# Negated row maxima and their rounded parts made by four reduce operations

## The chip, the core and the metric

The kernel runs on one core of a Trainium2 chip. The metric is the device time of one execution in microseconds (us). A core has five engines that run their own instruction streams and wait for each other through semaphores: TensorE (PE, matmuls; PEld are its weight loads), VectorE (DVE), ScalarE (ACT), GpSimd (POOL) and SyncE (SP, which here issues DMAs). SBUF is the on-chip working memory, PSUM the memory that matmuls write. In the profile L12 is line 12 of the kernel.

## What is computed

The reference mixes two branches of the same shape by a gate. Branch A is a Fourier transform of x (2048 x 512), written as matmuls; branch B is multi-head attention with 32 heads of 16 columns.

```python
def _A_ref(x, dft_seq_re, dft_seq_im, dft_hid_re, dft_hid_im):
    a = jnp.einsum("bsd,ed->bse", x, dft_hid_re)
    b = jnp.einsum("bsd,ed->bse", x, dft_hid_im)
    y = jnp.einsum("ts,bse->bte", dft_seq_re, a) - jnp.einsum("ts,bse->bte", dft_seq_im, b)
    return y

def _B_ref(x, wqkv, wo):
    ...
    scores = jnp.einsum("bhqd,bhkd->bhqk", q, k) * scale
    p = _softmax(scores, axis=-1)
    o = jnp.einsum("bhqk,bhkd->bhqd", p, v)
    return (lambda x, *d: x.transpose(*d))(o, 0, 2, 1, 3).reshape(B, S, D) @ wo

x = A_x
g = _sigmoid((x * gate_w).sum(-1, keepdims=True))
a = _A_ref(x, A_dft_seq_re, A_dft_seq_im, A_dft_hid_re, A_dft_hid_im)
b = _B_ref(x, B_wqkv, B_wo)
return g * a + (1 - g) * b
```

The attention weights are scaled so that the scores are large. The softmax therefore needs the true maximum of each row of scores before the exponential.

## The kernel before

Numbers that must be exact are carried as two float32r parts, a rounded one and the rest, so that three matmuls make one exact product.

The 32 heads are 16 pairs. For a pair p the queries and keys stand in the tiles `qs` and `ks` (two buffers each, p % 2), 64 rows for each head of the pair: 48 rows hold the parts of q or k, and two more rows of `qs`, 48 and 49 within each head's half, hold the negated row maximum in two parts, against rows of ones in `ks`. So a score matmul of a later step already delivers score minus maximum, and ScalarE only takes the exponential.

Each pair goes through two passes over its scores. In the first, `a_tile` (L285) multiplies 128 queries by 512 keys into a PSUM tile `a` (L291), and VectorE reduces it to one maximum per query (L293), into `mx`. After the 64 tiles of half a pair (`hf`, 1024 queries of both heads), two steps are put on a list, `deferred` (L297): `m_parts` and `m_rows`. `m_parts` takes the maximum over the four key blocks, negated, into `nm` (L302), its float32r rounding into `nhl[:, 0]`, and the rest into `nhl[:, 1]`. `m_rows` transposes the 32 numbers of each partition (L313) and sends them by eight DMAs (L319) into the two rows of `qs`. In the second pass `scores` (L778) makes the scores less their maximum (L791) with keys across the partitions, and the exponential `pt` (L792). `pv` (L825) multiplies it by the values into the PSUM tile `acc` (L839), and `evacuate` (L807) copies `acc` and adds it up on POOL (L819).

All of this runs woven into branch A. A section, `segment` (L946), takes its order from a written pattern: `d` matmuls (L465) of the Fourier branch on one half of the TensorE's rows, beside `a` and `s` matmuls on the other half, and at `|` the value matmuls. The long middle part is made of 192 sections with the pattern FULL (L916), each with 8 `a` tiles, 8 `s` tiles and two calls of `pv` at its end. PSUM banks are given by number in that pattern. An `a` matmul waits until the bank it writes was read by VectorE (L293) or by ScalarE (L792).

At the end of a FULL section (L990) everything deferred is run at once, and `full_now` is true: all of `m_parts` goes to VectorE, where L306 makes the rounding as a maximum of a number with itself, and L309 the rest. In the other sections the same is split: the first reduce on VectorE, a cast (L308) and a subtraction on POOL, and the transpose one section or part later. There are 32 halves of pairs; 24 of them come to this point in FULL sections.

POOL's own work in the full sections: the split of the Fourier matrices into two parts (`c_split`, L449 a cast and L450 a subtraction, each over 128 x 512), the sum of value tiles (L819), in the second half of the branch a sum with an earlier result (L524), and four of the eight DMAs of `m_rows`. Its instructions run in the order in which they were written. The transpose waits for the eight DMAs that read the same `mt` buffer before; an instruction with many waits is preceded by EVENT_SEMAPHORE instructions of its engine's queue, two waits each.

Of the kernel before, what the change touches and what calls it, by code (L numbers as in the profile page):

```python
# [9 lines left out]
F32 = mybir.dt.float32  # L10
F32R = mybir.dt.float32r
AF = mybir.ActivationFunctionType  # L12
ALU = mybir.AluOpType
AX = mybir.AxisListType

P = 128
# [15 lines left out]
def mix_kernel(ctx: ExitStack, tc: tile.TileContext, xa_t, xa, wqkv, w_hid, w_seq, wo, gate_w, out):  # L32
# [5 lines left out]
    nc = tc.nc  # L38
# [32 lines left out]
    const = ctx.enter_context(tc.tile_pool(name="const", bufs=1))  # L71
# [19 lines left out]
    ng = const.tile([P, NT], F32, name="ng")  # L91
    omg = const.tile([P, NT], F32, name="omg")
    mx = [const.tile([P, 2, NT, 4], F32, name=f"mx{i}") for i in range(2)]
    nm = [const.tile([P, 16], F32, name=f"nm{i}") for i in range(2)]
    nhl = [const.tile([P, 2, 16], F32R, name=f"nhl{i}") for i in range(2)]
    mt = [const.tile([P, 32], F32, name=f"mt{i}") for i in range(2)]

# [184 lines left out]
    full_now = False  # L282
    a_left = {}

    def a_tile(i, h, ps=None, bank=None):  # L285
        p, j = divmod(i, 64)
        qt, kb = divmod(j, 4)
        if ps is None:
            ps = psA.tile([P, 512], F32, "a", bank)
        r = slice(64 * h, 64 * h + (64 if p else 48))  # L290
        nc.tensor.matmul(ps, qs[p % 2][r, qt * P:(qt + 1) * P], ks[p % 2][r, kb * 512:(kb + 1) * 512],  # L291
                         start=True, stop=True)
        user = nc.vector.tensor_reduce(mx[p % 2][:, h, qt, kb:kb + 1], ps, AX.X, ALU.max)  # L293
        hf = j // 32
        a_left[p, hf] = a_left.get((p, hf), 64) - 1
        if not a_left[p, hf]:
            deferred.extend((partial(m_parts, p, hf), partial(m_rows, p, hf)))  # L297
        return user

    def m_parts(p, hf):  # L300

        nc.vector.tensor_reduce(nm[hf].rearrange("p (q h) -> p h q", h=2), mx[p % 2][:, :, 8 * hf:8 * hf + 8, :],  # L302
                                AX.X, ALU.max, negate=True)
        t = nhl[hf]
        if full_now:
            nc.vector.tensor_tensor(t[:, 0], nm[hf], nm[hf], ALU.max)  # L306
        else:
            nc.gpsimd.tensor_copy(t[:, 0], nm[hf])  # L308
        (nc.vector if full_now else nc.gpsimd).tensor_tensor(t[:, 1], nm[hf], t[:, 0].bitcast(F32), ALU.subtract)  # L309

    def m_rows(p, hf):

# [568 lines left out]
    for hf in range(2):  # L881
        for ct in range(4):
            n = 3 if hf and ct == 3 else 4
# [11 lines left out]
    one, two, three = [(psD, "d")], [(psS, "s"), (psD, "d")], [(psS, "s"), (psA, "a"), (psD, "d")]  # L895
# [195 lines left out]
```

## Time and profile before

| | us |
|---|---|
| median of three runs | 1675.19 (1674.93 to 1675.42) |
| the profiled execution | 1675.2 |
| its span, first to last instruction | 1673.4 |
| TensorE busy | 1663.6 (99% of the span) |
| VectorE busy | 1383.1 (83%) |
| ScalarE busy | 1242.9 (74%) |
| POOL busy | 660.1 (39%) |

The page groups instructions by source line, with their count, busy time, mean duration and the idle time ahead of them. Other views give single instructions in order of time (start and duration in us, then engine, line, operation, output tile and input tiles, shapes), the minimum, median and maximum duration of one line's instructions, and the busy time of every engine in a stretch of the span. VectorE operations that need nothing from each other overlap by some 0.08 us in the records, so a start is read against the next start rather than against an end. The granted TensorE clock is 0.999 of full speed in the mean.

### The profile page before, as it was taken

What the parts mean: (1) busy time and instruction counts of PE and PEld (TensorE: products, weight loads), DVE (VectorE), ACT (ScalarE), POOL (GpSimd) and SP (SyncE); (2) the same over time, 40 slices, a digit from 0 to 9 for tenths busy, and PEclk for the clock granted to TensorE, in tenths of its full rate; (3) what the DMA queues carried; (4) which work ended last, traced back from release to release, by engine and by line L of the source; (5) the groups of instructions that cost most, each with busy time, mean ns of one, the idle gap of its engine ahead of it and who ended that gap; (6) DMA issues with size and microseconds to landing.
All of it is one profiled execution on the core that took longest, in us unless ns stands there. A gap on an engine that the chain in (4) does not pass through costs nothing.

```text
span 1673.4 us, 34595 instructions
## 1 busy us (share of the span) xinstructions
PE 1663.6 (99%) x13040; PEld 1023.8 (61%) x13040; DVE 1383.1 (83%) x2337; ACT 1242.9 (74%) x2423; POOL 660.1 (39%) x688
## 2 busy tenths in 40 slices
PE   9999999999999999999999999999999999999998
PEld 7888855556666666656665665655665666545544
DVE  5439888888888888888888888888888888888954
ACT  5212377788888878887888787877888888788886
POOL 0202112234444456444444466554545456421110
PEclk9999999999999999999999999999999999999999
DMA  8963610414141443414156434324142535452114
GB/s 291 348 157 122 176 19 2 70 33 84 45 91 46 75 113 78 91 45 84 39 97 247 95 112 109 73 63 77 52 84 65 105 103 121 140 184 40 38 30 140
DMA packets 82689, 166.70 MB, mean 100 GB/s; under 512 B 19664, under 2 KB 20158, under 8 KB 78510
## 3 DMA queue, kind: packets, MB, share of 16 engines
q1 hardware_dynamic: 78282, 163.53, 38.5%
q8 instruction: 103, 1.69, 0.5%
q0 software_dynamic: 3808, 0.30, 0.2%
q14 instruction: 64, 0.52, 0.1%
q10 hardware_dynamic: 432, 0.66, 0.1%
HBM read 109.14 MB, written 54.65 MB: 98 GB/s over the span
## 4 chain that ended last, share of the span: by engine, by line
PE 98%; DVE 1%; DMA 0%; ACT 0%; issue 0%; DVEq 0%
PE acc L839 27%; PE d L465 27%; PE a L291 17%; PE s L791 14%; PE s L379 3%; PE s L411 1%; PE acc L799 1%; PE d L379 1%; PE s L106 1%; PE a L106 1%; PE a L108 1%; PE s L108 1%; PE s L107 1%; PE a L107 1%; DVE mx L293 1%; PE s L465 1%
## 5 line engine op out<-in xcount | busy, mean ns | idle before, releaser
L293 DVE TENSOR_REDUCE mx<-a 128x1 f32<-128x512 f32 x2026 | 1256.5, 683 | 177.3 <-PE a L291 151.8
L792 ACT ACTIVATE pt<-s 128x512 f32<-128x512 f32 x2006 | 1023.4, 622 | 70.9 <-PE s L791 59.9
L291 PE MATMUL a<-ks,qs 64*128 64x512 f32 (+1 forms) x2026 | 726.7, 405 | 2.2 <-DVE mx L293 2.2
L791 PE MATMUL s<-qs,ks 64*128 64x512 f32 (+1 forms) x2006 | 690.4, 400 | 0.0
L465 PE MATMUL d<-xab,ch 64*128 64x512 f32 x2016 | 645.9, 395 | 0.0
L291 PEld LDWEIGHTS a<-ks,qs 64*128 64x128 f32 (+1 forms) x2026 | 366.3, 184 | 217.2 <-issue 128.7
L839 PE MATMUL acc<-pt,vt 128*17 128x512 f32 (+1 forms) x3968 | 486.7, 598 | 0.0
L819 POOL TENSOR_TENSOR oe<-oe,part 128x512 f32<-128x512 f32 x169 | 218.3, 1292 | 507.7 <-ACT part L818 502.6
L791 PEld LDWEIGHTS s<-qs,ks 64*128 64x128 f32 (+1 forms) x2006 | 365.6, 185 | 55.1 <-issue 16.8
L465 PE MATMUL d<-xab,cl 64*128 64x512 f32 x1008 | 397.9, 395 | 0.0
L465 PEld LDWEIGHTS d<-xab,ch 64*128 64x128 f32 x2016 | 367.1, 184 | 26.5
L818 ACT COPY part<-acc 128x512 f32<-128x512 f32 x169 | 99.2, 587 | 183.0 <-PE acc L839 181.1
L839 PEld LDWEIGHTS acc<-pt,vt 128*17 128x17 f32 (+1 forms) x3968 | 91.6, 101 | 214.3 <-issue 151.5
L465 PEld LDWEIGHTS d<-xab,cl 64*128 64x128 f32 x1008 | 185.9, 184 | 13.7
L450 POOL TENSOR_TENSOR cl<-craw,ch 128x512 fp32r<-128x512 f32 x126 | 162.1, 1286 | 10.1
L465 PE MATMUL d<-wre,xab 64*128 64x512 f32 x336 | 90.5, 402 | 0.0
L449 POOL CAST ch<-craw 128x512 fp32r<-128x512 f32 x126 | 76.8, 609 | 16.5 <-PE s L791 14.4
L465 PEld LDWEIGHTS d<-wre,xab 64*128 64x128 f32 x336 | 58.9, 185 | 38.7 <-issue 23.3
L319 POOL DMA_DIRECT2D qs<-mt x119 | 67.0, 568 | 27.0 <-PE a L291 9.5
L465 PE MATMUL d<-wo_hl,o_hl 64*128 64x512 f32 (+1 forms) x246 | 68.2, 409 | 0.0
L465 PEld LDWEIGHTS d<-wo_hl,o_hl 64*128 64x128 f32 (+1 forms) x246 | 42.3, 185 | 29.7 <-issue 12.1
L483 POOL CAST xab<-y 128x512 fp32r<-128x512 f32 x16 | 9.8, 611 | 127.3 <-ACT y L481 99.1
(172 smaller groups left out, 1042.7 us busy)
## 6 DMA issues: line engine op xcount, KB each, us to landing
craw<-w_seq SPq DMA_DIRECT2D x128, 256.0 KB
qk<-hl SPq DMA_DIRECT2D x32, 512.0 KB
qs<-qk SPq DMA_DIRECT2D x96, 128.0 KB
ks<-qk SPq DMA_DIRECT2D x96, 128.0 KB
b<-hl SPq DMA_DIRECT2D x16, 512.0 KB
xab<-b SPq DMA_DIRECT2D x16, 512.0 KB
o<-oe SPq DMA_DIRECT2D x62, 128.0 KB
oh<-nh SPq DMA_DIRECT2D x12, 512.0 KB
```

The lines of the kernel that those rows point to most:

```text
L291: nc.tensor.matmul(ps, qs[p % 2][r, qt * P:(qt + 1) * P], ks[p % 2][r, kb * 512:(kb + 1) * 512], start=True, stop=True)
L293: user = nc.vector.tensor_reduce(mx[p % 2][:, h, qt, kb:kb + 1], ps, AX.X, ALU.max)
L319: (nc.gpsimd if own else nc.sync).dma_start(rows.rearrange("v (q b c) -> v b q c", q=8, b=4)[:, b], mt[hf][32 * b + h:32 * b + 32:2])
L379: i = nc.tensor.matmul(ps, st[r], mv[r], start=not half and not j, stop=half == 1 and j == 11)
L449: nc.gpsimd.tensor_copy(h1, raw)
L450: nc.gpsimd.tensor_tensor(l1, raw, h1.bitcast(F32), ALU.subtract)
L465: i = nc.tensor.matmul(self.ps, st[r], mv[r], start=not self.begun, stop=stop)
L791: nc.tensor.matmul(ps, ks[p % 2][rr, kt * P:(kt + 1) * P], qs[p % 2][rr, q0:q0 + 512], start=True, stop=True)
L792: return nc.scalar.activation(pts[u][:, 2 * qb + h], ps, AF.Exp, bias=0.0, scale=DH ** -0.5)
L818: nc.scalar.copy(part[0], acc)
L819: nc.gpsimd.tensor_tensor(total, total, part[0], ALU.add)
L839: i = nc.tensor.matmul(acc[32 * j:32 * j + width], v[:, 16 * h:16 * h + width], pt[:, j], start=begin, stop=done or close)
```

## The change

`nm` gets a second column. In the FULL sections `m_parts` reduces `mx` three times: negated into the first column of `nm` (float32), not negated and rounded to float32r into the second column, and negated and rounded into `nhl[:, 0]`. A fourth reduce adds the two columns: minus the maximum plus its rounding, which is the rest, into `nhl[:, 1]`. L306 and L309 are gone. In the other sections the work stays as it was, but reads the first column of the wider `nm`. In the instruction streams as built, the second and the third reduce carry no wait, the fourth waits for the second, and the transpose waits for the fourth and for the same DMAs as before. Line numbers behind this place grow by four.

```diff
-    nm = [const.tile([P, 16], F32, name=f"nm{i}") for i in range(2)]
+    nm = [const.tile([P, 16, 2], F32, name=f"nm{i}") for i in range(2)]
...
     def m_parts(p, hf):
 
-        nc.vector.tensor_reduce(nm[hf].rearrange("p (q h) -> p h q", h=2), mx[p % 2][:, :, 8 * hf:8 * hf + 8, :],
-                                AX.X, ALU.max, negate=True)
-        t = nhl[hf]
+        m, n, t = mx[p % 2][:, :, 8 * hf:8 * hf + 8, :], nm[hf], nhl[hf]
+        parts = [(n[:, :, 0], True)]
         if full_now:
-            nc.vector.tensor_tensor(t[:, 0], nm[hf], nm[hf], ALU.max)
+            parts += [(n[:, :, 1].bitcast(F32R), False), (t[:, 0], True)]
+        for out, negate in parts:
+            nc.vector.tensor_reduce(out.rearrange("p (q h) -> p h q", h=2), m, AX.X, ALU.max, negate=negate)
+        if full_now:
+            with nc.allow_low_precision(reason="two terms, rounded once"):
+                nc.vector.tensor_reduce(t[:, 1], n, AX.X, ALU.add)
         else:
-            nc.gpsimd.tensor_copy(t[:, 0], nm[hf])
-        (nc.vector if full_now else nc.gpsimd).tensor_tensor(t[:, 1], nm[hf], t[:, 0].bitcast(F32), ALU.subtract)
+            nc.gpsimd.tensor_copy(t[:, 0], n[:, :, 0])
+            nc.gpsimd.tensor_tensor(t[:, 1], n[:, :, 0], t[:, 0].bitcast(F32), ALU.subtract)
```

## The prediction

> **What bounds the kernel now.** I read the page first, then the waits of TensorE, then the lines of the changed helper, then its surroundings in order of time, and last the length of the stretches that hold it. Page and TensorE waits:
>
> ```profile
> span 1673.4 us, 34595 instructions
> ...
> PE 98%; DVE 1%; DMA 0%; ACT 0%; issue 0%; DVEq 0%
> ...
> PE a L291 <- DVE mx L293: 2.2, 4, 0.6
> ```
>
> TensorE sets the end: 98% of the chain that ended last is its own. The only VectorE work it is seen waiting for in the long middle part is the row maximum of a score tile (L293), four times, 2.2 us in all. A busy TensorE can still run slower than it might, so what a late maximum really costs is taken from lengths below, not from this idle time.
>
> The lines that the change touches, each with min/median/max in ns:
>
> ```profile
> L302 DVE TENSOR_REDUCE nm<-mx x32: 207/209/221, 171.7 to 1609.6; 128x16 f32<-128x64 f32 x32
> L306 DVE TENSOR_TENSOR nhl<-nm x24: 174/175/1041, 367.6 to 1431.0; 128x16 fp32r<-128x16 f32 x24
> L309 DVE TENSOR_TENSOR nhl<-nm,nhl x24: 174/175/519, 367.8 to 1432.1; 128x16 fp32r<-128x16 f32 x24
> L313 DVEq EVENT_SEMAPHORE  x115: 21/50/50, 280.9 to 1609.8; - x115
> L313 DVE STREAM_TRANSPOSE mt<-nhl x32: 200/211/214, 174.2 to 1610.8; 128x32 f32<-128x32 f32 x32
> ```
>
> The reduce and the transpose always take the same time; the two two-input operations, 16 numbers per partition, take 175 ns or up to six times that. Two of the 24 places in order of time (start, duration; VectorE, then VectorE and POOL of the second):
>
> ```profile
> 413.43 0.21 DVE L302 TENSOR_REDUCE nm<-mx 128x16 f32<-128x64 f32 x1
> 413.67 0.18 DVE L306 TENSOR_TENSOR nhl<-nm 128x16 fp32r<-128x16 f32 x1
> 413.88 0.18 DVE L309 TENSOR_TENSOR nhl<-nm,nhl 128x16 fp32r<-128x16 f32 x1
> 414.28 0.21 DVE L313 STREAM_TRANSPOSE mt<-nhl 128x32 f32<-128x32 f32 x1 [0.23 <-DMA craw<-w_seq]
> 414.42 3.69 DVE L293 TENSOR_REDUCE mx<-a 128x1 f32<-128x512 f32 x6
> ```
>
> ```profile
> 1012.99 0.21 DVE L302 TENSOR_REDUCE nm<-mx 128x16 f32<-128x64 f32 x1
> 1013.24 1.04 DVE L306 TENSOR_TENSOR nhl<-nm 128x16 fp32r<-128x16 f32 x1
> 1014.31 0.52 DVE L309 TENSOR_TENSOR nhl<-nm,nhl 128x16 fp32r<-128x16 f32 x1
> 1014.86 0.21 DVE L313 STREAM_TRANSPOSE mt<-nhl 128x32 f32<-128x32 f32 x1
> 1015.00 3.68 DVE L293 TENSOR_REDUCE mx<-a 128x1 f32<-128x512 f32 x6
> ```
>
> ```profile
> 1012.96 1.28 POOL L524 TENSOR_TENSOR y<-y,yr 128x512 f32<-128x512 f32 x1
> 1014.19 0.61 POOL L449 CAST ch<-craw 128x512 fp32r<-128x512 f32 x1
> ```
>
> In the second, L306 ends at 1014.28, 0.04 us after POOL's L524 (1014.24); L309 starts inside POOL's cast and ends at 1014.83, 0.03 us after it (1014.80). L302 ran wholly inside L524 and kept its 0.21. So a small two-input operation that meets a running POOL operation lasts until that one ends, and a one-input reduce does not.
>
> What a late L293 costs TensorE, in lengths from the start of one section's value matmuls (L839) to the next section's. The columns are stretch, us, then busy time by engine:
>
> ```profile
> 371.53:411.82 40.29, 40.29 (x338) 24.44 (x337) 34.76 (x57) 32.64 (x65) 17.06 (x17) 1.00 0.47 80
> 411.82:417.61 5.79, 5.79 (x50) 3.77 (x48) 5.49 (x13) 4.64 (x10) 3.33 (x6) 1.00 0.16 51
> 457.92:463.91 5.99, 5.99 (x50) 3.41 (x49) 5.69 (x13) 5.38 (x11) 5.35 (x8) 1.00 0.46 137
> 734.61:740.62 6.01, 6.01 (x51) 3.44 (x49) 5.71 (x13) 5.39 (x11) 5.38 (x8) 1.00 0.45 137
> 873.08:879.05 5.97, 5.97 (x51) 3.42 (x49) 5.67 (x13) 5.35 (x11) 5.33 (x8) 1.00 0.44 134
> 1011.40:1018.22 6.82, 6.26 (x51) 3.42 (x49) 6.72 (x13) 5.40 (x11) 6.62 (x8) 1.00 0.40 114
> 1150.58:1157.40 6.82, 6.26 (x51) 3.41 (x49) 6.72 (x13) 5.38 (x11) 5.45 (x7) 1.00 0.37 117
> 1157.40:1197.58 40.18, 40.18 (x337) 24.68 (x336) 34.77 (x57) 32.65 (x65) 18.74 (x20) 1.00 0.18 54
> 1197.58:1203.74 6.16, 6.16 (x51) 3.48 (x49) 5.51 (x13) 4.77 (x10) 4.37 (x6) 1.00 0.16 46
> 1290.01:1296.82 6.81, 6.24 (x50) 3.40 (x48) 6.71 (x13) 5.37 (x11) 5.43 (x7) 1.00 0.36 113
> 1429.17:1435.95 6.78, 6.24 (x53) 3.42 (x51) 6.68 (x13) 5.34 (x11) 5.41 (x7) 1.00 0.23 79
> ```
>
> Seven sections without the helper last 40.29 us, 5.756 each (the section ends are those of the value matmuls in the order of time). Sections with it stand at every eighth place, 24 of them, as L306's count says. From the first reduce to the next L293 the helper holds VectorE for 0.99 us at 413.43 (section 5.79, excess 0.03) and for 2.01 at 1012.99 (section 6.82, excess 1.06): 1.02 later there, 1.03 longer the section. So up to about 0.95 us VectorE catches up (eight maxima of 0.6 us, from start to start, in 5.756), and beyond that each microsecond late is a microsecond of TensorE.
>
> **The change, part by part.** Call the start of the first reduce T. Now: L306 at T+0.24, L309 at T+0.45, transpose at T+0.85, next L293 at T+0.99. The 0.40 between L309 and the transpose is more than L309's 0.18: four of VectorE's semaphore waits (the L313 DVEq row) stand there, and they follow L309's issue whatever it takes. The built order has the same waits for the transpose after the change.
>
> *Removed:* L306 and L309, 24 times each. With them goes what seven of the 24 lose to POOL: 5.99 + 6.01 + 5.97 + 6.82 + 6.82 + 6.81 + 6.78 = 45.20, less 7 x 5.756 = 40.29, is 4.9 us. A little of it is given back today: the seven sections behind a long stall last 40.18 against 40.29, 0.11 less. Four long ones give at most 0.5; I take 0.3. Net 4.6.
>
> *Added:* two more reduces over the same 64 numbers (R2, R3) and one over 16 pairs (R4). R2 and R3 wait for nothing; R4 waits for R2, not for R3, which writes another tile. No row shows an independent small reduce behind a reduce in these sections; the nearest are these, and the gap L302 to L306 with a wait (0.24):
>
> ```profile
> 195.51 0.17 DVE L772 TENSOR_SCALAR ng<-g 128x16 f32<-128x16 f32 x1
> 195.59 0.17 DVE L773 TENSOR_SCALAR omg<-g 128x16 f32<-128x16 f32 x1
> ...
> 1478.08 0.22 DVE L302 TENSOR_REDUCE nm<-mx 128x16 f32<-128x64 f32 x1
> 1478.21 3.07 DVE L293 TENSOR_REDUCE mx<-a 128x1 f32<-128x512 f32 x5
> ```
>
> So a step is 0.08 at least and 0.24 at most; I take 0.13, since that row is the same reduce with an independent one behind it. R2 at T+0.13, R3 at T+0.26, R2 done at 0.13 + 0.24 = T+0.37, and the engine is free for R4 at T+0.39. R4 lasts between 0.17 and 0.21 (16 and 64 inputs), under the 0.40 of the four waits, so it costs nothing itself; were those waits gone, it would cost its 0.2. Transpose at T+0.79, next L293 at T+0.93: 0.06 before today's undisturbed case, though one operation more is issued. For the sixteen undisturbed sections (24 less the seven and the one below) that is worth what they still exceed 5.756 by, 0.03 in the row of 411.82: at most 16 x 0.03 = 0.5; I take 0.3.
>
> The Trainium skill speaks against this part: "VectorE: DVE Perf Modes", section "The DRAIN you can't avoid", says that the next operation does not start until the pipe is empty, and its "Rules for kernel authors" say to minimize the number of operations. By that rule the step would be the longer one and rival B would hold; the 0.13 row does not bear it out.
>
> *Kept:* the section at 1197.58 is 0.40 long with no stall of a two-input operation:
>
> ```profile
> 1199.64 0.17 DVE L309 TENSOR_TENSOR nhl<-nm,nhl 128x16 fp32r<-128x16 f32 x1
> 1200.39 0.21 DVE L313 STREAM_TRANSPOSE mt<-nhl 128x32 f32<-128x32 f32 x1 [0.58 <-DVE nhl L309]
> ```
>
> Its transpose comes 0.75 behind L309 instead of 0.40, so the waits between lasted longer. They stay; I count no gain there (bounds 0 and 0.4).
>
> The eight places outside the full sections keep their cast and subtraction on POOL, reading every other number of a wider tile, behind other work: nothing, and if uncovered some 0.2 us. The transposes' DMAs (four on SP and, where POOL issues, four there) start up to 0.9 us earlier in stalled places; POOL reaches its own only after L449, which ends at 1014.80 either way. Nothing else is moved past a queue.
>
> *Sum:* 4.6 + 0.3 = 4.9 us. The profiled execution took 1675.2 (1.8 outside its span), which is also the median of before: 1675.2 - 4.9 = **1670.3 us**.
>
> **The rivals.**
>
> *B, slower.* The four reduces run one behind the other, 0.24 apart. R4 at T+0.73, transpose at T+1.13, next L293 at T+1.27, 0.28 later than an undisturbed place today, so an excess of 0.31 in 24 sections, 7.4 us, against today's 4.6 + 24 x 0.03 = 5.3: 2.1 slower, **1677.3**. It decides once the next L293 is later than T+0.99 + 4.6/24 = T+1.18. For it: every dependent pair is 0.24 or 0.21 apart. Against: the 0.13 row.
>
> *C, the stall stays.* It is not the second SBUF input but the fp32r output that waits for POOL; R2, R3 and R4 write fp32r too. Then only the 0.3 is left: **1674.9**. For it: L306 and L309 write fp32r and the unharmed L302 does not, and no row shows a reduce that does. Against it, a two-input operation of another stage, with one input in PSUM (tile s) and an fp32r output, inside a POOL operation:
>
> ```profile
> 39.65 0.69 DVE L103 TENSOR_TENSOR hl<-s,hl 128x512 fp32r<-128x512 f32 x1 [0.45 <-ACT hl L102]
> 39.21 1.29 POOL L103 TENSOR_TENSOR wv<-raw,wv 128x512 fp32r<-128x512 f32 x1 [37.90 <-ACT wv L102]
> ```
>
> It ends at 40.34, before POOL's at 40.50, so the output alone does not wait. The Trainium skill, "SBUF — State Buffer", section "SBUF: two separate sides", says the same in general: VectorE operations with two SBUF inputs or in a two-port mode take the pair of ports shared with GpSimd, whole operation against whole operation. By it C falls; for a reduce that writes fp32r no run here shows it yet.
>
> *D, half overlap.* R4 midway between T+0.39 and T+0.73: next L293 at T+1.10, 0.11 later, 24 x 0.11 = 2.6 lost of 4.6: 2.0 gained, **1673.2**.
>
> **How the numbers follow.** Chances: forecast 0.70, B 0.07, C 0.06, D 0.12, and 0.05 for what I don't see, most of it slower. The forecast's own range goes from everything at 5.756 with nothing given back and the 0.4 gone too (4.9 + 0.5 + 0.4 = 5.8, 1669.4) to 1671.6, where the step is 0.17. To hold 8 in 10 it must take in D: 1669.0 to 1674.0. A change of 0.2% (3.4 us, what can be told apart here) is reached by the forecast and the better edge of D: faster 0.72. C, B's centre and most of D are within it: 0.22. Slower by more: 0.06, from B with a longer step and the unseen.
>
> **What would show it.** In the profile after: no small VectorE operation in these places over 0.25 us; R2 and R3 0.13 apart; R4 near T+0.39; transpose 0.40 behind it; next L293 near T+0.93; the stretches that begin with the seven stalled sections at 5.76 to 5.80; TensorE's 2.2 us of waiting for L293 gone. Wrong would be reduces of 0.4 to 1 us (C), starts 0.24 apart (B), a stall that moves to the transpose, or sections at 5.76 with the time lost after the full sections instead.

## The result and the profile after

| | before | changed |
|---|---|---|
| median of 8 runs, us | 1675.06 (1674.55 to 1675.5) | 1670.16 (1669.9 to 1670.3) |
| span of the profiled execution, us | 1673.4 | 1668.1 |

The ratio of the changed kernel's time to the one before is 0.997, with a 95% interval of 0.9961 to 0.9979: 4.9 us faster, as forecast (1670.3).

From the page of the changed kernel, the chain that ended last; and TensorE's waits in the list of waits:

```profile
PE 99%; DMA 0%; DVE 0%; DVEq 0%; issue 0%
...
PE d L178 <- DVE xab L173: 1.1, 1, 1.1
PE s L243 <- DVE xab L164: 0.2, 1, 0.2
```

TensorE now waits for VectorE only at the start of the kernel; the row with L293, 2.2 us, is gone. The small operations, line by line (count, then min/median/max in ns; L307 has the first three reduces, L310 the fourth, L317 is the transpose that was L313):

```profile
L307 DVE TENSOR_REDUCE nm<-mx x56: 208/211/222, 171.3 to 1604.1; 128x16 f32<-128x64 f32 x32, 128x16 fp32r<-128x64 f32 x24
L307 DVE TENSOR_REDUCE nhl<-mx x24: 205/208/211, 367.3 to 1426.6; 128x16 fp32r<-128x64 f32 x24
L310 DVE TENSOR_REDUCE nhl<-nm x24: 178/179/184, 367.4 to 1426.7; 128x16 fp32r<-128x32 f32 x24
L317 DVE STREAM_TRANSPOSE mt<-nhl x32: 199/211/214, 173.8 to 1605.4; 128x32 f32<-128x32 f32 x32
```

None exceeds 222 ns in any place, with fp32r outputs or without; 37 of these reduces ran wholly inside a POOL operation. The section that stood first among the long ones, in order of time (VectorE, then POOL; two reduces are merged in the first row):

```profile
1012.15 0.34 DVE L307 TENSOR_REDUCE nm<-mx 128x16 f32<-128x64 f32 x2
1012.40 0.20 DVE L307 TENSOR_REDUCE nhl<-mx 128x16 fp32r<-128x64 f32 x1
1012.53 0.18 DVE L310 TENSOR_REDUCE nhl<-nm 128x16 fp32r<-128x32 f32 x1
1012.89 0.21 DVE L317 STREAM_TRANSPOSE mt<-nhl 128x32 f32<-128x32 f32 x1 [0.18 <-DVE nhl L310]
1013.03 0.65 DVE L293 TENSOR_REDUCE mx<-a 128x1 f32<-128x512 f32 x1
```

```profile
1012.13 1.29 POOL L528 TENSOR_TENSOR y<-y,yr 128x512 f32<-128x512 f32 x1
```

POOL's sum runs from 1012.13 to 1013.42 and covers all of it, and every operation keeps its length. The next maximum starts 0.88 us behind the first reduce; it was 2.01. In most of the 24 places it is 0.91. The first rows below show one of them; in the rows behind, at 459, the transpose comes late and the maximum with it, 1.28 us behind the first reduce:

```profile
413.03 0.34 DVE L307 TENSOR_REDUCE nm<-mx 128x16 f32<-128x64 f32 x2
...
413.94 0.65 DVE L293 TENSOR_REDUCE mx<-a 128x1 f32<-128x512 f32 x1
```

```profile
459.13 0.34 DVE L307 TENSOR_REDUCE nm<-mx 128x16 f32<-128x64 f32 x2
...
459.50 0.18 DVE L310 TENSOR_REDUCE nhl<-nm 128x16 fp32r<-128x32 f32 x1
460.27 0.21 DVE L317 STREAM_TRANSPOSE mt<-nhl 128x32 f32<-128x32 f32 x1 [0.59 <-DVE nhl L310]
460.41 1.25 DVE L293 TENSOR_REDUCE mx<-a 128x1 f32<-128x512 f32 x2
```

The same stretches as before (us, then busy times by engine):

```profile
365.39:1430.49 1065.10, 1065.10 (x8883) 644.80 (x8881) 935.33 (x1607) 867.84 (x1697) 543.63 (x552) 1.00 0.38 87
...
411.44:417.20 5.76, 5.76 (x50) 3.55 (x48) 5.54 (x14) 4.59 (x10) 3.30 (x6) 1.00 0.17 51
457.52:463.60 6.08, 6.08 (x50) 3.39 (x48) 5.49 (x14) 5.36 (x11) 5.44 (x8) 1.00 0.47 135
734.10:739.86 5.76, 5.76 (x51) 3.56 (x49) 5.55 (x14) 5.17 (x11) 5.12 (x8) 1.00 0.50 143
780.11:786.18 6.07, 6.07 (x51) 3.41 (x49) 5.50 (x14) 4.80 (x10) 4.26 (x6) 1.00 0.13 46
872.48:878.23 5.75, 5.75 (x51) 3.58 (x49) 5.53 (x14) 5.17 (x11) 5.13 (x8) 1.00 0.43 139
1010.57:1016.35 5.78, 5.78 (x50) 3.57 (x48) 5.55 (x14) 5.19 (x11) 5.57 (x6) 1.00 0.25 93
1148.68:1154.43 5.75, 5.75 (x50) 3.53 (x48) 5.52 (x14) 5.16 (x11) 4.38 (x5) 1.00 0.25 93
1154.43:1194.77 40.34, 40.34 (x339) 24.07 (x337) 34.78 (x57) 32.79 (x65) 19.80 (x22) 1.00 0.21 61
1194.77:1200.53 5.76, 5.76 (x51) 3.59 (x49) 5.54 (x14) 4.59 (x10) 3.98 (x6) 1.00 0.18 47
1286.77:1292.50 5.73, 5.73 (x50) 3.52 (x49) 5.50 (x14) 5.14 (x11) 4.37 (x5) 1.00 0.30 92
1424.72:1430.49 5.77, 5.77 (x51) 3.50 (x49) 5.54 (x14) 5.17 (x11) 4.41 (x5) 1.00 0.28 92
```

The four sections that had 6.78 to 6.82 us have 5.73 to 5.78. Two of the three with 6.0 have 5.76 and 5.75; the third, at 457.52, has 6.08, and so has one at 780.11 (6.07) that had been undisturbed. The one that had 6.16 without a stall is at 5.76. From the first of the 24 sections to the end of the last: 1065.10 us in the first row, against

```profile
365.70:1435.95 1070.25, 1068.02 (x8885) 652.56 (x8883) 940.18 (x1583) 868.74 (x1697) 544.67 (x554) 1.00 0.38 87
```

in the kernel before: 5.15 of the 5.3 us between the two spans.

### The profile page after: what moved, and what is told of

Same layout as the page of the kernel before. It is cut to its first block, busy times and chain, and to the rows that moved or that the text cites. A ratio compares the mean times of both kernels' runs of the same rounds, so it can differ in the third digit from the quotient of the medians.

```text
span 1668.1 us, 34619 instructions
## 1 busy us (share of the span) xinstructions
PE 1660.8 (100%) x13040; PEld 1012.7 (61%) x13040; DVE 1378.0 (83%) x2361; ACT 1242.1 (74%) x2423; POOL 660.1 (40%) x688
## 4 chain that ended last, share of the span: by engine, by line
PE 99%; DMA 0%; DVE 0%; DVEq 0%; issue 0%
PE acc L843 28%; PE d L469 25%; PE a L291 18%; PE s L795 15%; PE s L383 3%; PE s L415 1%; PE d L383 1%; PE acc L803 1%; PE a L108 1%; PE a L107 1%; PE s L108 1%; PE s L107 1%; PE a L106 1%; PE s L106 1%; PE s L469 1%; PE a L469 1%
## 5 line engine op out<-in xcount | busy, mean ns | idle before, releaser
L293 DVE TENSOR_REDUCE mx<-a 128x1 f32<-128x512 f32 x2026 | 1257.0, 683 | 178.0 <-PE a L291 153.7
```

## The experiments

Theory W at the start: a small VectorE operation with two SBUF inputs that meets a running POOL operation lasts until that one ends; a reduce does not; what is then late beyond a section's slack of some 0.95 us is TensorE's time one for one. Rivals: the number of operations (N), the fp32r output (O). O had already fallen with the profile after, whose reduces write fp32r beside POOL in 0.21 us. Times are medians; the kernel before ran beside them with 1674.8 to 1675.2 us.

### Half the change

The rounding by a reduce that waits for nothing, the rest by the two-input subtraction.

```diff
-            parts += [(n[:, :, 1].bitcast(F32R), False), (t[:, 0], True)]
+            parts += [(t[:, 0], True)]
...
-                nc.vector.tensor_reduce(t[:, 1], n, AX.X, ALU.add)
+            nc.vector.tensor_tensor(t[:, 1], n[:, :, 0], t[:, 0].bitcast(F32), ALU.subtract)
```

> Half of the change: the rounding is made by a second reduce, the rest again by a two-input subtraction. Theory W (a VectorE operation with two SBUF inputs that meets a running POOL operation lasts until that one ends; a reduce does not): the subtraction starts 0.37 us behind the first reduce, is 0.18 us long in most places and about 0.9 us in the four places that stand beside POOL's sum with the earlier result; the four sections are about 0.5 us longer than the others, so 2.0 us are given back: 1672.2 us (1671.5 to 1673). Rival N (what counts is the number of small operations and their order, not their inputs): one operation fewer than in the changed kernel, so 1670 us or less and no long section. Rival O (the small float32r output waits): the reduce that writes float32r would be long in the same four places, too, and the time near 1674.

Measured: 1672.3 us, ratio 0.9982 (0.9973 to 0.9991). The section beside POOL's sum (here L527), VectorE, then POOL, and its length:

```profile
1012.52 0.21 DVE L307 TENSOR_REDUCE nhl<-mx 128x16 fp32r<-128x64 f32 x1
1012.76 0.91 DVE L309 TENSOR_TENSOR nhl<-nm,nhl 128x16 fp32r<-128x16 f32 x1
...
1012.35 1.28 POOL L527 TENSOR_TENSOR y<-y,yr 128x512 f32<-128x512 f32 x1
```

```profile
1010.80:1017.03 6.23, 6.22 (x51) 3.39 (x49) 6.16 (x13) 5.36 (x11) 6.05 (x7) 1.00 0.31 91
```

With one operation fewer than the changed kernel it is 2.1 us slower. The reduce that writes fp32r keeps 0.21 inside POOL's sum; the subtraction ends at 1013.67, 0.04 behind POOL's 1013.63. The other three places beside that sum have 6.23 to 6.26 us, too. N and O are out here.

### The same without POOL's sum

```diff
-                nc.gpsimd.tensor_tensor(y, y, yr[0], ALU.add)
```

> The half change (rounding by a reduce, rest by a two-input subtraction) without POOL's sum of the two halves of the Fourier result, so that the first half is missing in the output. Theory W2 (the small subtraction waits for the POOL operation that is running): in the four places where it was 0.9 us beside that sum, POOL now runs its 0.61 us cast from the section's end on, the subtraction is 0.2 to 0.3 us, ends under the waits ahead of the transpose, and the four sections are 5.75 instead of 6.24 us: 2.0 us less than the half change, 1670.3 us (1669.5 to 1671). Rival (the place itself is slow, whatever POOL does): 0.9 us and 6.24 us as before, 1672.3 us.

Measured: 1669.33 us, ratio 0.9968 (0.9956 to 0.9981). The subtraction, and the first of the four sections; the others have 5.77, 5.75 and 5.73 us:

```profile
L309 DVE TENSOR_TENSOR nhl<-nm,nhl x24: 174/174/269, 367.2 to 1426.4; 128x16 fp32r<-128x16 f32 x24
```

```profile
1009.83:1015.67 5.84, 5.84 (x51) 3.64 (x49) 5.54 (x13) 5.22 (x11) 5.68 (x8) 1.00 0.43 135
```

Its longest is 269 ns instead of 914, and the long sections are gone: POOL's operation was the cause, not the place. The time is 0.2 us under the stated range. From the first of the 24 sections to the end of the last it is 1.9 us shorter than the half change (2.0 expected); the other 1.1 us between the two spans (1670.8 and 1667.8) lie outside that stretch, and what the missing sum is worth there was not followed up.

### A cast in place of the two-input rounding, in the kernel before

```diff
-            nc.vector.tensor_tensor(t[:, 0], nm[hf], nm[hf], ALU.max)
+            nc.vector.tensor_copy(t[:, 0], nm[hf])
```

> The kernel before, with the rounding made by a cast (one SBUF input, 16 numbers) instead of a maximum of a number with itself; the two-input subtraction behind it stays. Theory W (the second SBUF input is what waits for POOL): the cast is 0.18 us everywhere, the subtraction starts 0.45 behind the reduce and ends with POOL's operation; four sections of about 6.3 instead of 6.8 us and three of 5.8 instead of 6.0: 1672.2 us (1671.5 to 1673). Theory W2 (a second SBUF port is what waits, and a float32 copy from SBUF to SBUF uses it too): the cast is as long as the operation it replaces, 1 us in the same four places, and the time is that of before, 1675 us.

Measured: 1675.19 us, ratio 1.0 (0.9991 to 1.0009). The cast (ns), and one place with POOL beside it:

```profile
L306 DVE CAST nhl<-nm x24: 174/175/1048, 367.7 to 1431.0; 128x16 fp32r<-128x16 f32 x24
...
1012.99 1.05 DVE L306 CAST nhl<-nm 128x16 fp32r<-128x16 f32 x1
...
1012.71 1.29 POOL L524 TENSOR_TENSOR y<-y,yr 128x512 f32<-128x512 f32 x1
```

It has one SBUF input and waits just like the operation with two. Theory W as stated was too narrow, and the time is the one W2 gives: the reduces and the transpose do not wait, a copy does. That it is a second port that they wait for is argued; a trace shows the waiting alone. The Trainium skill, "SBUF — State Buffer", section "SBUF: two separate sides", counts VectorE operations in a two-port mode among those that lock the pair of ports shared with GpSimd, and says that a float32 copy from SBUF to SBUF runs in such a mode. If the cast here does, which no trace shows, its length is what that rule gives.

### One more operation: a reduce, or a two-input one

Both write a tile that nobody reads, ahead of the fourth reduce.

```diff
+            nc.vector.tensor_reduce(more, m, AX.X, ALU.max)
```

> The changed kernel with one more small reduce, of the same 64 numbers, into a tile that nobody reads, ahead of the fourth reduce. Theory W: it costs 0.13 us in each of 24 places, next maximum at 1.04 instead of 0.91 us behind the first reduce, of which about 0.08 is over the slack: 2 us, 1672.2 us (1671 to 1673), no long place. Rival N (the number of operations counts as such): 24 times 0.24, 1676 us.

```diff
+            nc.vector.tensor_tensor(more, m[:, :, :, 0], m[:, :, :, 0], ALU.max)
```

> The same place as in the run with one more small reduce, but the added operation is a maximum of two equal SBUF inputs of 16 numbers into a tile that nobody reads. Theory W: 0.09 us in most places, but until POOL's running operation ends in the four places beside POOL's sum with the earlier result (some 0.9 us) and a little in the three beside POOL's subtraction: 4 times 0.8, 3 times 0.2 and 0.05 in the rest, 1674.8 us (1673.5 to 1676), over 1.5 us more than with the added reduce. Rival N: less than with the added reduce, since 16 numbers take less than 64: 1671.5 us.

Measured: 1669.2 us (1669.14 to 1670.65; ratio 0.9967, 0.9954 to 0.9979) with the reduce, 1672.1 us (ratio 0.9982, 0.9973 to 0.9991) with the two-input operation. The order is that of theory W, 2.9 us apart, but they are 3.0 and 2.7 us under their numbers, and both below their ranges. The added reduce, in order of time:

```profile
413.21 0.34 DVE L308 TENSOR_REDUCE nm<-mx 128x16 f32<-128x64 f32 x2
413.46 0.21 DVE L308 TENSOR_REDUCE nhl<-mx 128x16 fp32r<-128x64 f32 x1
413.58 0.21 DVE L310 TENSOR_REDUCE more<-mx 128x16 f32<-128x64 f32 x1
413.71 0.18 DVE L312 TENSOR_REDUCE nhl<-nm 128x16 fp32r<-128x32 f32 x1
413.98 0.21 DVE L319 STREAM_TRANSPOSE mt<-nhl 128x32 f32<-128x32 f32 x1
414.12 1.25 DVE L294 TENSOR_REDUCE mx<-a 128x1 f32<-128x512 f32 x2
```

The fourth reduce starts at 0.50 instead of 0.38, and yet the next maximum at 0.91 as without the addition. The four semaphore waits ahead of the transpose begin 0.39 us behind the first reduce in both kernels. So they do not follow the start of the fourth reduce; they seem to begin when it is handed to the engine, as soon as the second has signalled. The added reduce therefore moves only what runs under these waits and is free. Against the changed kernel (1669.9 to 1670.3) its time is not told apart.

The added two-input operation is free in the same way in most places, which is where theory W had it too dear. Beside POOL's sum it lasts 0.89 to 0.93 us, and the four sections have 6.33 to 6.39 us, some 0.6 more than 5.756 instead of the 0.8 expected. A fifth place was not foreseen. There it starts 0.11 us behind POOL's subtraction (here L456) and ends 0.04 behind it, at 966.96; VectorE, POOL and the section:

```profile
965.73 1.23 DVE L310 TENSOR_TENSOR more<-mx 128x16 f32<-128x16 f32 x1
...
965.62 1.29 POOL L456 TENSOR_TENSOR cl<-craw,ch 128x512 fp32r<-128x512 f32 x1
```

```profile
963.73:970.45 6.72, 6.28 (x51) 3.42 (x49) 6.69 (x15) 4.84 (x10) 6.64 (x9) 1.00 0.16 41
```

In the changed kernel that section has 5.77 us. The added operation writes float32, so here, too, the fp32r output is not what waits.

### The reduces one behind the other

```diff
+    def after_last(i, made):
+        if made:
+            tc.add_manual_dep(i.ins, made[-1].ins.name,
+                              mybir.DependencyInfo(mybir.DependencyClass.Sync, mybir.DependencyReason.DATA))
+        return i
...
+            made.append(after_last(i, made))
...
+                after_last(nc.vector.tensor_reduce(t[:, 1], n, AX.X, ALU.add), made)
```

> The changed kernel with each of the four reduces made to wait for the one before. Nothing is left out. Theory W with the slack of the section (about 0.95 us from the first small reduce to the next maximum, beyond it one for one): starts 0.24 apart, transpose at 1.13, next maximum 1.27 us behind the first reduce, about 0.3 us more in each of 24 sections: 1677 us (1676 to 1678), slower than the kernel before. Rival (the starts do not matter because TensorE has slack of its own): 1670 to 1671 us.

Measured: 1678.2 us, ratio 1.0018 (1.0009 to 1.0027). One place and its length:

```profile
414.08 0.47 DVE L313 TENSOR_REDUCE nm<-mx 128x16 f32<-128x64 f32 x2
414.58 0.22 DVE L313 TENSOR_REDUCE nhl<-mx 128x16 fp32r<-128x64 f32 x1
...
415.38 1.25 DVE L293 TENSOR_REDUCE mx<-a 128x1 f32<-128x512 f32 x2
```

```profile
412.49:418.59 6.10, 6.10 (x51) 3.41 (x49) 5.78 (x14) 4.78 (x10) 3.64 (x6) 1.00 0.19 49
```

Starts are 0.25 apart, the next maximum is 1.30 behind the first reduce, and the section has 6.10 us, 0.34 over 5.756. The time is 0.2 us over the stated range, 8.0 above the changed kernel, and slower than before. This is rival B's chain: the four reduces pay because only one of them waits for another.

### The 0.3 us that two sections still lose

Counting VectorE's recorded instructions in order of their starts, the lost time of the changed kernel lies behind number 703 (457.52) and number 1215 (780.11), both among the waits ahead of the transpose (the rows at 459 above show the first); in the kernel before it lay behind number 1855 (the section of 6.16 us). Divided by 128, all three leave 63. Eleven or sixteen one-column memsets near the start, where VectorE waits for data, move everything behind them:

```diff
+        for i in range(11):
+            nc.vector.memset(more[:, i:i + 1], 0.0)
```

> The changed kernel with 11 one-column memsets of VectorE near the start, where it waits for its first data; everything later on VectorE moves by 11 places in its stream. Theory P (the 0.35 us that two helper places of the changed kernel still lose is lost at every 128th instruction of VectorE's stream, and is seen where that falls among the semaphore waits ahead of the transpose): with 11 no boundary falls there, all 24 sections are 5.73 to 5.80 us, 0.6 us less: 1669.5 us. Rival T (lost to something at a point in time, a DMA or POOL): the same two sections stay at 6.06 to 6.08 us, 1670.2 us.

> The same with 16 memsets. Theory P: three boundaries fall among the waits ahead of the transpose, in the 8th, 15th and 22nd of the 24 sections (first reduce near 689.7, 1012 and 1334 us), each about 6.07 us, and none in the 3rd and 10th: 0.3 us over the changed kernel, 1670.5 us. Rival T: the 3rd and 10th as in the changed kernel, 1670.2 us.

Measured: 1669.93 us (1668.89 to 1670.74) with 11, 1670.62 us (1670.1 to 1671.37) with 16. The 3rd and 10th sections with 11; then the 8th, 15th and 22nd with 16, whose 3rd and 10th have 5.76 and 5.73 us:

```profile
458.59:464.35 5.76, 5.76 (x51) 3.56 (x49) 5.54 (x14) 5.15 (x11) 5.11 (x8) 1.00 0.50 141
781.04:786.78 5.74, 5.74 (x51) 3.52 (x49) 5.52 (x14) 4.56 (x10) 3.93 (x6) 1.00 0.13 48
```

```profile
687.81:693.84 6.03, 6.03 (x51) 3.43 (x49) 5.46 (x14) 4.75 (x10) 3.55 (x6) 1.00 0.19 49
1010.66:1016.74 6.08, 6.08 (x51) 3.50 (x49) 5.52 (x14) 5.42 (x11) 5.86 (x7) 1.00 0.32 93
1333.33:1339.38 6.05, 6.05 (x51) 3.39 (x49) 5.51 (x14) 4.77 (x10) 4.74 (x7) 1.00 0.18 47
```

Theory P holds: the loss goes with the place in the stream, to exactly the three sections named beforehand, and T falls. As a gain it is not shown. The version with 11 has no long section (all 24 have 5.73 to 5.78 us), but its time is not told apart from the changed kernel's, and 0.4 us over its number. In its profile the 24 sections together are some 0.75 us shorter than in the changed kernel, while the 23 stretches between them grew from 926.36 to 927.03 us; with 16 they have 927.07. Why they grew is open.

## Why the prediction was right

*The removal.* The seven stalled sections had 45.20 us; they now have 6.08 + 5.76 + 5.75 + 5.78 + 5.75 + 5.73 + 5.77 = 40.62, 4.6 less, and 4.9 were it not for the 6.08, which has another cause. That POOL's running operation was what they waited for is shown by leaving it out. The traces of the kernel before, the cast, the half change with and without the sum and the added two-input operation hold 168 such small operations: 49 start inside a POOL operation, and each ends 0.03 to 0.09 us behind it; the other 119 take 174 to 183 ns.

*The price of a late maximum.* The slack of some 0.95 us holds in the other runs, too: with the next maximum 0.91 us behind the first reduce the section has 5.76 us, with 1.28 it has 6.08, with 1.30 in the serial version 6.10, and it had 6.82 with 2.01.

*The added reduces.* Start to start 0.13 between the first two (two merged rows of 0.21 last 0.34), the fourth at 0.38 (forecast 0.39), the next maximum at 0.91 (0.93), the fourth reduce 0.18 long. The 0.13 step carried the forecast: with 0.25 the same four reduces make the kernel slower than before. The prediction read "VectorE: DVE Perf Modes" (the Trainium skill, section "The DRAIN you can't avoid") as speaking against this step, but the same paragraph goes on: "A next op that is not held starts earlier". The trace agrees with that: 0.13 us between reduces that wait for nothing, 0.25 where each waits. So rival B had less behind it than the prediction gave it. What that page's "Rules for kernel authors" (the Trainium skill) add, to minimize the number of operations and not of semaphores, the runs do not bear out: the same four reduces with three waits between them instead of one took 8.0 us more.

*What the forecast had too narrow.* It put the stall on the second SBUF input. The cast shows that having one input doesn't save an operation. The sum was not touched by that, since all that replaced the pair were reduces.

*What it had wrong.* The step "Kept": the 0.40 us of one section was taken as something that stays there. It is gone from that section and stands at 0.32 and 0.31 in two others, because the helper has one VectorE instruction more and the boundaries fall elsewhere: 0.23 us more lost than booked. "Given back" is not shown: the three stretches behind a long stall had 40.28, 40.18 and 40.22 us and now have 40.25, 40.34 and 40.29, while the other stretches of before range from 40.23 to 40.34 anyway. All 23 together grew by 0.15 us (926.21 to 926.36), where 0.3 was booked. The sixteen undisturbed sections were mis-sized: they had 92.68 us together, 0.6 above 16 x 5.756, and all but the one of 6.07 have lost that; 0.3 was booked, and at most 0.5, from a single row. The upper edge of 1671.6 for a step of 0.17 does not follow from the prediction's own terms either: the next maximum at T+1.05 is 0.06 late 24 times, 1.4 of the 4.6, which gives 1672.0.

*How much of the hit is luck.* The terms as measured are 4.9 for the removal and 0.6 for the undisturbed sections, less 0.15 and 0.23: 5.1 us, which but for rounding is the 5.15 between the two traces. The forecast had 4.9, and so have the medians. The mechanism and the main term are right; the errors of the small terms partly cancel. That the medians meet the forecast to 0.2 us is partly chance, since the runs of the kernel before alone lie 0.95 us apart.

## What to carry to other kernels

Look at the spread of one line's durations, not at its mean: 175 ns with a maximum of 1041 was a wait for another engine here, and the end of the other engine's operation beside it named it. A small VectorE reduce could take the place of a two-input operation where POOL is busy. Small reduces that wait for nothing cost 0.13 us each from start to start, those that wait for the one before 0.25, so one operation more can still be the shorter chain.

## What the runs showed of the hardware

- A VectorE copy of 16 numbers per partition, float32 to fp32r, SBUF to SBUF, waits for a running POOL operation (up to 1048 ns), as a two-input operation does; reduces of 32 to 64 numbers and a 32-column transpose don't (at most 225 ns in the runs above).
- Some 0.35 us is lost behind a VectorE instruction whose number among the recorded ones leaves 63 after division by 128, and it was seen only where it falls among the semaphore waits ahead of a transpose: elsewhere the next maximum mostly follows at its usual 0.6 us. Not every such place showed it: behind number 1727 of the changed kernel, between the fourth reduce and the first wait, nothing was lost. What causes the loss was not measured.
- Semaphore waits of VectorE's queue stand 0.1 us apart. The four ahead of the transpose hid the whole fourth reduce, and with one reduce more they still hid it although it ran 0.12 us later (0.50 to 0.68 us behind the first reduce, transpose at 0.77).
